# A three-stage attention and mixer kernel: decoding raw 64-bit weights in rows of 512 columns instead of 256

## Chip, cores and metric

One core of one Trainium2 chip runs the whole kernel as one program. The metric is the device time of an execution in microseconds (us). Three runs of the kernel before took 825.0, 825.81 and 827.83 us; the median is 825.81 us.

## What is computed

The reference has three stages on a tensor of 4 batches, 768 positions and 512 channels. The first is a chunked local attention (8 heads of 64 channels, 8 memory keys). The second is a gated mixture of 4 causal attention experts. The third, which the change touches, is a mixer and a two-layer network:

```python
xt = x.transpose(0, 2, 1)
h = xt @ U @ V
u = x + h.transpose(0, 2, 1)
ch = np.maximum(u @ w_ch1, 0.0) @ w_ch2       # w_ch1: 512 x 2048, w_ch2: 2048 x 512
return (u + ch).astype(np.float32)
```

`U`, `V`, `w_ch1` and `w_ch2` are 64-bit floats, which reach the chip as raw bits: two 32-bit words for each element.

## The kernel before, in words

**Numbers.** Nearly every product is made from two parts of each factor: a rounded high part (`hi`, type fp32r) and the remainder (`lo`). A product is three matmuls: lo by hi, hi by lo, hi by hi.

**Decode.** A raw weight is fetched as pairs of words (L130, or ahead of time by `fetch`, L140) and rebuilt into fp32 by `decode` (L126): one ScalarE activation scales the high word (L134), and three VectorE operations shift it (L135), put in the sign (L136) and the low bits (L137). `decode_split` (L157) then makes `hi` by a ScalarE copy (L159) and `lo` by a subtraction (L160) on VectorE, or on GpSimd for `w2`. Everything goes in pieces of 128 partitions by DC = 256 columns, two pieces to a weight row of 512.

**First layer.** Because the second attention's output projection `wo` stands in front of `w_ch1`, `fuse_w1` (L264) multiplies `woT` into `w_ch1` on the chip: for each of 4 column blocks j and each of 4 row blocks kt, two halves, each with 6 matmuls of 256 columns (L275), 192 in all. The result is split into `wp_h`, `wp_l` (L285, L286), the weights of the first layer (`product1`, L310). `load_wt` (L257) loads and splits `woT` by `split_load` (L250) in four pieces of 256.

**Second layer.** For the first FA = 4 row blocks of `w_ch2` it is a plain product: `load_w2` (L192) decodes and splits them, `gemm1` (L321) makes the relu of the first layer, and `gemm2` (L329) multiplies; sums go through `o` tiles to DRAM (`save_part`, L335). The other 12 row blocks are taken in pairs f = 4, 6, 8, 10, 12, 14, and with `wo` itself as a seventh pair (RES = 16), by a seven-product scheme for 2 by 2 blocks: `load_pair` (L198) decodes four blocks of 256 into one tile `hd`, and makes seven left factors from them (sums or differences, L216, then hi and lo, L218 and L219), `right` (L953) makes seven right factors, `multiply` (L1047) the products (L1053), and `OUTPUTS` says how they are added up.

**Stages.** Batch by batch, the two attentions run in rounds (`rnd`, L755). During the last batch's rounds (from about 310 us) the third stage begins behind them: `load_wt`, `fuse_w1` for j = 0, `load_w2`, and `early` (L343), the plain products of the first two column chunks, with pairs 4 and 6 (`fill`, L819). When attention has ended (about 422 us), the plain products of the other four chunks run, and `rest` (L935) makes the remaining weights beside them; from about 510 us to the end the seven-product scheme runs.

**Order.** The program is written in order of priority; a planner with a simulated timeline then fixes each engine's own order of instructions and each wait. An engine's queue runs in that order: a waiting instruction holds up those behind it. `issue_after` ties an instruction behind another in the plan, and `take(generator, n)` places so many steps of background work behind a round. All DMAs go through SP's queue.

**Buffers.** A tile with a tag shares that tag's `bufs` buffers and waits until one is free. Those that matter here: `d_t` (decode target, ND0 = 2 in the pool `dp0`), `d_r` (raw `woT`, 2), `raw64` (raw words), `hh` and `hl` (NHP = 4 each, used first for words fetched ahead, then for `gemm1`'s results), `w2h0` to `w2l3` (one each), `o` (2). `raw1` of kt = 0 isn't fetched ahead: it is decoded through `raw64` of `dp0`, a pool that is there from the start.

Of the kernel before, what the change touches and what calls it, by code (L numbers as in the profile page):

```python
# [23 lines left out]
DM = H * D  # L24
# [3 lines left out]
KT = DM // 128  # L28
# [32 lines left out]
ND0, NW0, ND1, NW1 = 2, 2, 6, 3  # L61
LATE = 12
NHP = 4
# [9 lines left out]
NSW = 3  # L73
# [8 lines left out]
NDE = 3  # L82
# [5 lines left out]
                ((0, 0), (0, 1), ADD), ((1, 0), (0, 0), SUB), ((0, 1), (1, 1), SUB))  # L88
# [3 lines left out]
           (((0, 0), ADD), ((1, 0), ADD)), (((0, 0), SUB), ((0, 1), ADD)), (((1, 1), ADD),), (((0, 0), ADD),))  # L92
# [5 lines left out]
def tile_chunk_attention__moe_attention__mixer(  # L98
# [22 lines left out]
    def f32(ap):  # L121
        return ap.bitcast(F32)
# [24 lines left out]
    def fetch_w1():  # L147
        for kt in range(1, KT):
            for i, hc in enumerate(halves):
                raw1[kt, i] = fetch(w1[kt, 0][:, hc], 'hh' if i else 'hl')  # L150

    def fetch_w2():
        for f in range(FA):
            for i, cs in enumerate(halves):
                raw2[f, i] = fetch(w2[f][:, cs], "hh" if i else "hl")
# [25 lines left out]
    nd, nw, nh, ns = [ND0], [NW0], [2], [NSW]  # L181
# [10 lines left out]
    def load_w2(f):  # L192
        w2h[f] = pa.tile([128, DM], F32R, name=f"w2h{f}", tag=f"w2h{f}", bufs=1)
        w2l[f] = pa.tile([128, DM], F32R, name=f"w2l{f}", tag=f"w2l{f}", bufs=1)
        for i, cs in enumerate(halves):
            decode_split(w2[f][:, cs], w2h[f][:, cs], w2l[f][:, cs], raw2.pop((f, i)), nc.gpsimd)

    def load_pair(f):  # L198
# [29 lines left out]
    def sum_tile():  # L228
        if in_b[0]:
            return dp0.tile([128, DC], F32, name="sw0", tag="w1_h", bufs=NW0)  # L230
        return dp.tile([128, DC], F32, name="sw", bufs=ns[0])

    def factor_tiles(f):

        if f < LATE:
            t = [(ea if f in EPAIRS else wp2).tile([128, 2, DC], F32R, name=f"sw{f}_{n}") for n in range(7)]
        elif f == LATE:
            t = [pa.tile([128, 2, DC], F32R, name=f"sw{f}_{n}", tag=f"w2{'hl'[n % 2]}{n // 2}", bufs=1) for n in range(7)]
        elif f == RES:
            t = [dp0.tile([128, 2, 2, DC], F32R, name=f"swr{n}", tag=f"wp_{n}0", bufs=1) for n in "hl"]  # L240
            t = [x[:, i] for x in t for i in range(2)]
            t += [ea.tile([128, 2, DC], F32R, name=f"swr{n}", tag="o", bufs=2) for n in range(2)]
            t += [pa.tile([128, 2, DC], F32R, name="swr2", tag="w2l3", bufs=1)]
        else:
            t = [pa.tile([128, 2, DC], F32R, name=f"sw{f}_{n}", tag="h" + "hl"[n % 2], bufs=NHP) for n in range(7)]
        return [(x[:, 0], x[:, 1]) for x in t]

    in_b = [False]
# [15 lines left out]
    def fuse_w1(ps, j, tag):  # L264

        acc = [ps.tile([128, 512], F32, name="w1p", **tag) for _ in range(2)]
        for kt in range(KT):
            for i, hc in enumerate(halves):
                w1_h = dp.tile([128, DC], F32R, name="w1_h", tag="w1_h", bufs=nw[0])
                w1_l = dp.tile([128, DC], F32R, name="w1_l", bufs=nw[0])  # L270
                decode_split(w1[kt, j][:, hc], w1_h, w1_l, raw1.pop((kt, i), None) if j == 0 else None)
                for pr in range(2):
                    cs = slice(pr * 128, (pr + 1) * 128)
                    for n, (w, x) in enumerate(((wt["l"], w1_h), (wt["h"], w1_l), (wt["h"], w1_h))):
                        nc.tensor.matmul(acc[pr][:, hc], w[:, kt, cs], x, start=(kt == 0 and n == 0 and i == 0),  # L275
                                         stop=(kt == KT - 1 and n == 2 and i == 1))
                if i == 0:
                    yield
            if kt < KT - 1:
                yield  # L280
# [54 lines left out]
    def save_part(po, c, m):  # L335
        o = ea.tile([128, CT], F32, name="o", tag="o", bufs=2)
# [28 lines left out]
    with ExitStack() as p1:  # L365
# [446 lines left out]
        def close_proj():  # L812
# [4 lines left out]
            nd[0], nw[0], nh[0], ns[0] = NDE, 1, NHE, NSE  # L817
# [110 lines left out]
    nd[0], nw[0], nh[0], ns[0] = ND1, NW1, 2, NSW  # L928
    with ExitStack() as p2:
# [49 lines left out]
        for c in late:  # L979
            nxt = c + 1 if c + 1 < NCH else None  # L980
            po = [ps.tile([128, CT], F32, name=f"po{m}", tag=f"po{m}", bufs=1) for m in range(KT)]
            for f in range(FA):
# [6 lines left out]
                if nxt is None and f == FS:  # L989
# [4 lines left out]
                    dp, in_b[0], nd[0], nw[0] = dp0, True, ND0, NW0  # L994
# [177 lines left out]
```

## Time and profile before

| | |
|---|---|
| median of three runs | 825.81 us |
| profiled execution, its own time | 825.71 us |
| its span, first to last instruction | 823.9 us |
| PE (TensorE matmul) busy | 795.0 us, 96% |
| DVE (VectorE) busy | 626.0 us, 76% |
| ACT (ScalarE) busy | 502.1 us, 61% |
| POOL (GpSimd) busy | 157.5 us, 19% |
| matmul line of `fuse_w1` (L275) in the chain that ended last | 2% |

The span is 1.8 us shorter than the execution's own time; that remainder lies around it. A busy share is an average over stages with different limits, so the rows below are taken stage by stage. PE's granted clock is 1.00 of full speed in every stretch used here.

### The profile page before, as it was taken

What the parts mean: (1) busy time and instruction counts of PE and PEld (TensorE: products, weight loads), DVE (VectorE), ACT (ScalarE), POOL (GpSimd) and SP (SyncE); (2) the same over time, 40 slices, a digit from 0 to 9 for tenths busy, and PEclk for the clock granted to TensorE, in tenths of its full rate; (3) what the DMA queues carried; (4) which work ended last, traced back from release to release, by engine and by line L of the source; (5) the groups of instructions that cost most, each with busy time, mean ns of one, the idle gap of its engine ahead of it and who ended that gap; (6) DMA issues with size and microseconds to landing.
All of it is one profiled execution on the core that took longest, in us unless ns stands there. A gap on an engine that the chain in (4) does not pass through costs nothing.

```text
span 823.9 us, 17920 instructions
## 1 busy us (share of the span) xinstructions
PE 795.0 (96%) x6388; PEld 717.2 (87%) x6388; DVE 626.0 (76%) x1982; ACT 502.1 (61%) x1476; POOL 157.5 (19%) x247
## 2 busy tenths in 40 slices
PE   7989999999999998899999999999999999999997
PEld 5879989989989897777878888999999999999996
DVE  4687868777677768888758699989587595784956
ACT  5787757767667745765536567665465464654652
POOL 2554434435243434441100000000000000000000
PEclk9999999999999999999999999999999999999999
DMA  9834523433233105133417544202103021030211
GB/s 287 222 117 144 169 64 96 148 104 112 64 102 104 43 2 191 47 111 115 141 36 272 179 154 158 74 1 89 41 1 128 1 78 51 1 129 1 78 52 52
DMA packets 38664, 81.53 MB, mean 99 GB/s; under 512 B 4400, under 2 KB 8496, under 8 KB 37808
## 3 DMA queue, kind: packets, MB, share of 16 engines
q1 hardware_dynamic: 38576, 80.39, 30.5%
q8 instruction: 51, 0.84, 0.4%
q14 instruction: 37, 0.30, 0.1%
HBM read 64.64 MB, written 15.73 MB: 98 GB/s over the span
## 4 chain that ended last, share of the span: by engine, by line
PE 76%; DVE 11%; DMA 5%; ACT 4%; issue 3%; POOL 1%; SPq 0%; DVEq 0%; ACTq 0%; POOLq 0%
PE acc L1053 24%; PE ph L317 15%; PE t L751 7%; PE pqk L532 6%; PE po L333 5%; PE pv L572 4%; PE s L473 4%; PE tpc L674 3%; PE sc L612 2%; PE w1p L275 2%; PE tp L501 2%; PE sc L613 2%; DMA raw<-in_w 1%; DMA k_t<-in_kw 1%; ACT ac L629 1%
## 5 line engine op out<-in xcount | busy, mean ns | idle before, releaser
L1053 PE MATMUL acc<-xhi,sw 128*128 128x256 f32 x1008 | 188.3, 282 | 0.1
L1053 PEld LDWEIGHTS acc<-xhi,sw 128*128 128x128 f32 x1008 | 159.3, 189 | 4.7 <-ACT xhi L971 0.3
L1053 PE MATMUL acc<-xlo,sw 128*128 128x256 f32 x504 | 139.0, 282 | 0.2 <-DVE xlo L972 0.2
L968 DVE TENSOR_TENSOR sx<-t 128x256 f32<-128x256 f32 x180 | 68.0, 424 | 68.2 <-ACT t L961 68.2
L961 ACT ACTIVATE t<-ph 128x512 f32<-128x512 f32 x72 | 43.1, 599 | 105.5 <-PE ph L317 105.5
L1053 PEld LDWEIGHTS acc<-xlo,sw 128*128 128x128 f32 x504 | 95.6, 190 | 2.5 <-DVE xlo L972 0.4
L654 POOL TENSOR_SCALAR ac<-ac,su,g 128x128 f32<-128x128 f32 (+5 forms) x92 | 66.9, 736 | 135.0 <-DVE su L652 50.0
L629 ACT ACTIVATE ac<-sc,nmc 128x128 f32<-128x128 f32 (+5 forms) x96 | 60.6, 635 | 43.2 <-DVE nmc L647 30.6
L971 ACT CAST xhi<-sx 128x256 fp32r<-128x256 f32 x205 | 74.7, 406 | 19.8 <-DVE sx L968 17.1
L480 ACT ACTIVATE a<-a,nm 128x96 f32<-128x96 f32 x192 | 69.9, 366 | 17.5 <-DVE nm L477 17.0
L972 DVE TENSOR_TENSOR xlo<-sx,xhi 128x256 fp32r<-128x256 f32 x205 | 77.3, 425 | 2.9 <-ACT xhi L971 2.3
L317 PE MATMUL ph<-zh,wp_l 128*128 128x512 f32 x192 | 61.2, 399 | 0.0
L317 PE MATMUL ph<-zh,wp_h 128*128 128x512 f32 x192 | 60.7, 394 | 0.0
L473 PE MATMUL s<-k_t,q_t 128*128 128x96 f32 x384 | 52.8, 275 | 6.2 <-DMA k_t<-in_kw 3.2
L473 PEld LDWEIGHTS s<-k_t,q_t 128*128 128x128 f32 x384 | 48.6, 193 | 8.8 <-DVE nm L477 4.0
L485 POOL TENSOR_TENSOR a<-a,rs 128x288 f32<-128x288 f32 x64 | 42.6, 667 | 71.7 <-DVE rs L484 34.8
L317 PE MATMUL ph<-zl,wp_h 128*128 128x512 f32 x176 | 56.1, 394 | 0.1
L674 PE MATMUL tpc<-ident_s,ac 128*128 128x128 f32 x336 | 51.7, 276 | 2.8 <-ACT ac L629 1.4
L612 PE MATMUL sc<-kl,qs 128*128 128x384 f32 (+2 forms) x144 | 48.3, 341 | 3.3 <-DVE ath L677 1.6
L477 DVE CUSTOM_DVE_ANT_0 a<-s,band_s 128x96 f32<-128x96 f32 x192 | 39.5, 251 | 14.6 <-PE s L473 14.1
L647 DVE TENSOR_REDUCE nmc<-sc 128x1 f32<-128x512 f32 (+2 forms) x48 | 39.0, 818 | 13.0 <-PE sc L616 12.5
L751 PE MATMUL t<-ath,vt 128*64 128x128 f32 x672 | 46.0, 276 | 1.9 <-DVE ath L677 1.7
(187 smaller groups left out, 1976.8 us busy)
## 6 DMA issues: line engine op xcount, KB each, us to landing
raw<-in_w SPq DMA_DIRECT2D x64, 256.0 KB, 3.5
q_t<-in_qT SPq DMA_DIRECT2D x32, 384.0 KB, 3.2
k_t<-in_kw SPq DMA_DIRECT2D x32, 288.0 KB, 3.7
v_t<-in_vw SPq DMA_DIRECT2D x32, 288.0 KB, 3.1
part<-o SPq DMA_DIRECT2D x24, 256.0 KB, 2.5
pt<-part SPq DMA_DIRECT2D x6, 1024.0 KB, 4.8
out<-pt SPq DMA_DIRECT2D x24, 256.0 KB, 2.3
zf<-zs SPq DMA_DIRECT2D x8, 512.0 KB, 4.9
```

Source lines behind the costliest of these rows:

```text
L317: nc.tensor.matmul(p, w[f // 4][:, pr, fs], z[:, pr], start=(n == 0), stop=(n == 5))
L473: last = nc.tensor.matmul(s[:, j, :], w["q"][:, qd * 3 + j], w["k"][:, qd * 3 + j], start=True, stop=True).ins
L480: nc.scalar.activation(a[:, j, :], a[:, j, :], AF.Exp, bias=nm[:, j:j + 1], scale=-1.0, accum_out=ss[:, j:j + 1])
L612: nc.tensor.matmul(s[:, o:o + w], q, kl[b, e, hf][:, :w], start=True, stop=False)
L629: nc.scalar.activation(aa[h][:, :n], src, AF.Exp, bias=nm[:, h:h + 1], scale=1.0, accum_out=su[:, h:h + 1])
L654: (nc.vector if ending[0] else nc.gpsimd).tensor_scalar(aa[h][:, :n], aa[h][:, :n], su[:, h:h + 1], gates[b, i // 3][:, i % 3, 2 * pr + h: ...
L674: hold['t', 6 * (i // 3) + 3 * pr + i % 3] = nc.tensor.transpose(tp[h][:, j * 128:(j + 1) * 128], aa[h][:, j * 128:(j + 1) * 128], ident_s ...
L751: session.append(nc.tensor.matmul(*a, **kw).ins)
L968: nc.vector.tensor_tensor(x, t[:, p[0], p[1]], t[:, q[0], q[1]], op=op)
L971: nc.scalar.copy(hi, x)
L972: nc.vector.tensor_sub(lo, x, f32(hi))
L1053: ended[0] = nc.tensor.matmul(acc[n][:, m], w[:, ms], x, start=(f == FA and u == 0 and m == 0), stop=(f == NF - 2 and u == 2 and m == 1)).ins
```

## The change

Raw rows are decoded 512 columns at a time. `fetch` takes whole rows; `raw1` now covers kt = 0 too. `d_t` of `dp0` becomes a 512 wide tile, and `split_load` uses the same two buffers for raw `woT`. `fuse_w1` makes 6 matmuls of 512 columns for each (j, kt), 96 in all; for j = 0 its `w1_h`, `w1_l` lie in the tiles that `w2h`, `w2l` take later. `gemm1` lays out its results in pairs of f, so that a pair of tiles has the size of a raw row (NHP goes from 4 to 2). For the pairs 4, 6, 8 and 10 `load_pair` decodes two rows instead of four blocks, and makes the left factors in four steps, three of them two factors wide; factor 6 changes its sign, and `OUTPUTS` takes it back. Pairs 12, 14 and 16 go as before. The `o` tiles become three.

```diff
-ND0, NW0, ND1, NW1 = 2, 2, 6, 3
+ND0, NW0, ND1, NW1, NR1, NRE = 2, 2, 3, 3, 3, 2
-NHP = 4
+NHP = 2
+NO = 3
-NSW = 3
+NSW = 2
-NDE = 3
+NDE = 2
...
     def fetch(src, tag):
-        raw = pa.tile([128, DC, 2], U32, name="raw", tag=tag, bufs=NHP)
+        raw = pa.tile([128, DM, 2], U32, name="raw", tag=tag, bufs=NHP)
...
     def fetch_w1():
-        for kt in range(1, KT):
-            for i, hc in enumerate(halves):
-                raw1[kt, i] = fetch(w1[kt, 0][:, hc], 'hh' if i else 'hl')
+        for kt in range(KT):
+            raw1[kt] = fetch(w1[kt, 0], 'hh' if kt % 2 else 'hl')
...
     def decode_split(src, hi, lo, raw=None, eng=None):
-        v = decode(dp, src, DC, raw=raw, bufs=nd[0])
+        t = dp.tile([128, DM], U32, name="d_t", bufs=nd[0])
+        v = decode(dp, src, DM, t, raw=raw, bufs=nr[0])
...
-        for i, cs in enumerate(halves):
-            decode_split(w2[f][:, cs], w2h[f][:, cs], w2l[f][:, cs], raw2.pop((f, i)), nc.gpsimd)
+        decode_split(w2[f], w2h[f], w2l[f], raw2.pop(f), nc.gpsimd)
...
+        if f < LATE:
+            for k in range(2):
+                row = hd[:, 2 * k:2 * k + 2].rearrange("p a c -> p (a c)").bitcast(U32)
+                decode(dp, w2[f + k], DM, row, bufs=nr[0])
+                yield
+            pool = ea if f in EPAIRS else wp2
+            for u, (ns_, x, y, op) in enumerate((((5, 6), hd[:, 1::2], hd[:, 0::2], SUB), ((4, 1), hd[:, 0:2], hd[:, 2:4], ADD),
+                                                 ((2, 3), hd[:, 0::3], None, None), ((0,), hd[:, 0:1], hd[:, 3:4], ADD))):
+                w = len(ns_)
+                z = pool.tile([128, 2, w, DC], F32R, name=f"sw{f}_{u}")
+                if op:
+                    v = dp.tile([128, 2, DC], F32, name="sw", bufs=ns[0])[:, :w]
+                    nc.vector.tensor_tensor(v, x, y, op=op)
+                else:
+                    v = x
+                nc.scalar.copy(z[:, 0], v)
+                nc.vector.tensor_sub(z[:, 1], v, f32(z[:, 0]))
...
     def split_load(src, hi, lo):
-        for cs in halves:
-            raw = dp.tile([128, DC], F32, name="d_r", bufs=nd[0])
-            nc.sync.dma_start(raw, src[:, cs])
-            nc.vector.tensor_copy(hi[:, cs], raw)
-            nc.gpsimd.tensor_sub(lo[:, cs], raw, f32(hi[:, cs]))
+        raw = dp.tile([128, DM], F32, name="d_r", tag="d_t", bufs=nd[0])
+        nc.sync.dma_start(raw, src)
+        nc.vector.tensor_copy(hi, raw)
+        nc.gpsimd.tensor_sub(lo, raw, f32(hi))
...
-            for i, hc in enumerate(halves):
-                w1_h = dp.tile([128, DC], F32R, name="w1_h", tag="w1_h", bufs=nw[0])
-                w1_l = dp.tile([128, DC], F32R, name="w1_l", bufs=nw[0])
-                decode_split(w1[kt, j][:, hc], w1_h, w1_l, raw1.pop((kt, i), None) if j == 0 else None)
-                for pr in range(2):
-                    cs = slice(pr * 128, (pr + 1) * 128)
-                    for n, (w, x) in enumerate(((wt["l"], w1_h), (wt["h"], w1_l), (wt["h"], w1_h))):
-                        nc.tensor.matmul(acc[pr][:, hc], w[:, kt, cs], x, start=(kt == 0 and n == 0 and i == 0),
-                                         stop=(kt == KT - 1 and n == 2 and i == 1))
-                if i == 0:
-                    yield
+            if j:
+                w1_h, w1_l = (dp.tile([128, DM], F32R, name=f"w1_{n}", bufs=NW1) for n in "hl")
+            else:
+                w1_h, w1_l = (pa.tile([128, DM], F32R, name=f"w1_{n}", tag=f"w2{n}{kt}", bufs=1) for n in "hl")
+            decode_split(w1[kt, j], w1_h, w1_l, None if j else raw1.pop(kt))
+            yield
+            for pr in range(2):
+                cs = slice(pr * 128, (pr + 1) * 128)
+                for n, (w, x) in enumerate(((wt["l"], w1_h), (wt["h"], w1_l), (wt["h"], w1_h))):
+                    nc.tensor.matmul(acc[pr], w[:, kt, cs], x, start=(kt == 0 and n == 0), stop=(kt == KT - 1 and n == 2))
...
-        hh = pa.tile([128, CT], F32R, name="hh", tag="hh", bufs=NHP)
-        hl = pa.tile([128, CT], F32R, name="hl", tag="hl", bufs=NHP)
+        if f % 2 == 0:
+            hs[c] = [pa.tile([128, 2, CT], F32R, name=n, tag=n, bufs=NHP) for n in ("hh", "hl")]
+        hh, hl = (x[:, f % 2] for x in hs[c])
```

## Rows read from the trace of the kernel before

**Rows 1.** Busy time by stretch: stretch, length, then PE, PEld, DVE, ACT, POOL busy, clock, DMA

```profile
85.00:110.00 25.00, 23.56 (x234) 21.90 (x232) 21.11 (x94) 18.52 (x68) 11.32 (x16) 1.00 0.41 129
310.00:365.00 55.00, 48.02 (x378) 41.20 (x378) 48.06 (x125) 35.51 (x103) 26.82 (x39) 1.00 0.31 101
365.00:420.00 55.00, 52.76 (x357) 42.93 (x354) 43.15 (x93) 28.78 (x67) 6.97 (x7) 1.00 0.38 123
420.00:800.00 380.00, 379.92 (x2532) 347.80 (x2531) 293.70 (x777) 215.31 (x518) 0.00 (x0) 1.00 0.24 83
```

**Rows 2.** Timeline of PE, 310 to 420 us, matmuls that waited: first, costliest, last of 17

```profile
313.20 0.33 PE L612 MATMUL sc<-kl,qs 128*128 128x128 f32 x1 [1.56 <-DVE ath L677]
...
341.35 0.30 PE L674 MATMUL tpc<-ident_s,ac 128*128 128x128 f32 x1 [1.37 <-ACT ac L629]
...
415.71 1.31 PE L751 MATMUL t<-ath,vt 128*64 128x128 f32 x20 [0.18 <-DVE ath L677]
```

**Rows 3.** Chain that ended last, in order of time: start, us, what and how many

```profile
422.70 2.78 PE ph L317 x12
...
427.84 4.11 PE po L333 x18
...
442.54 1.91 PE w1p L275 x16
...
512.88 1.40 PE ph L317 x6
```

**Rows 4.** Groups by line and shape: count, busy us, mean ns of one, idle before

```profile
L326 DVE SCALAR_TENSOR_TENSOR hl<-ph,hh 128x512 fp32r<-128x512 f32 x24 | 16.5, 691 | 6.6 <-ACT hh L325 6.4
L136 DVE SCALAR_TENSOR_TENSOR d_t<-raw,d_t 128x256 uint32<-128x256 uint32 x40 | 17.7, 452 | 0.3
L134 ACT ACTIVATE d_t<-raw 128x256 f32<-128x256 f32 x40 | 16.8, 437 | 6.9 <-DVE w_l L160 2.7 <-DVE hl L326 2.2 <-issue 0.7
L160 DVE TENSOR_TENSOR w_l<-d_t,w_h 128x256 fp32r<-128x256 f32 x32 | 13.5, 432 | 1.4 <-ACT w_h L159 1.3
L135 DVE TENSOR_SCALAR d_t<-d_t 128x256 uint32<-128x256 uint32 x40 | 13.4, 337 | 4.4 <-ACT d_t L134 4.3
L159 ACT CAST w_h<-d_t 128x256 fp32r<-128x256 f32 x32 | 12.5, 407 | 6.8 <-PE w1p L275 4.3 <-DVE d_t L137 1.5 <-DVE su L652 0.9
L134 ACT ACTIVATE hd<-raw 128x256 f32<-128x256 f32 x24 | 10.0, 433 | 10.5 <-DMA raw<-in_w 10.3
L160 POOL TENSOR_TENSOR w2l<-d_t,w2h 128x256 fp32r<-128x256 f32 x8 | 6.2, 775 | 5.2 <-ACT w2h L159 5.2
L410 POOL TENSOR_TENSOR wvg_l<-raw,wvg_h 128x520 fp32r<-128x520 f32 x2 | 2.6, 1306 | 0.0
L405 ACT CAST wqk_h<-raw 128x512 fp32r<-128x512 f32 x4 | 2.4, 610 | 2.6 <-DMA raw<-in_wqk 2.6
```

**Rows 5.** Timeline of all engines, 84 to 104 us, around the decode of kt = 0

```profile
92.48 0.43 DVE L136 SCALAR_TENSOR_TENSOR d_t<-raw,d_t 128x256 uint32<-128x256 uint32 x1
...
94.11 0.56 DVE L552 SCALAR_TENSOR_TENSOR qs<-pqk,qs 64x384 fp32r<-64x384 f32 x1
...
94.81 0.94 PE L532 MATMUL pqk<-xl,wqk_h 128*128 128x384 f32 x4 [0.67 <-DVE qs L552]
```

**Rows 6.** Timeline of all engines, 308 to 325 us: decode of kt = 1, then the split of woT

```profile
311.90 0.52 DVE L135 TENSOR_SCALAR d_t<-d_t 128x256 uint32<-128x256 uint32 x1 [0.78 <-ACT d_t L134]
...
312.34 0.81 DVE L677 COPY ath<-tpc 128x640 f32<-128x640 f32 x1
...
321.47 1.42 POOL L255 TENSOR_TENSOR wt_l<-d_r,wt_h 128x256 fp32r<-128x256 f32 x2 [3.09 <-DVE wt_h L254]
```

**Rows 7.** Timeline of all engines, 335 to 368 us: first-layer weights of j = 0

```profile
337.68 1.11 ACT L285 CAST wp_h<-w1p 128x512 fp32r<-128x512 f32 x2
...
354.15 1.27 DVE L286 TENSOR_TENSOR wp_l<-w1p,wp_h 128x512 fp32r<-128x512 f32 x2
```

More of the change, by code (lines that the diff above doesn't have):

```diff
@@ L180, in tile_chunk_attention__moe_attention__mixer @@
     dp0 = dp = pass_b.enter_context(tc.tile_pool(name="dp0", bufs=1, side="right"))
-    nd, nw, nh, ns = [ND0], [NW0], [2], [NSW]
+    nd, nr, nh, ns = [ND0], [1], [2], [NSW]
     DC = 256
@@ L194, in load_w2 @@
         w2l[f] = pa.tile([128, DM], F32R, name=f"w2l{f}", tag=f"w2l{f}", bufs=1)
-        for i, cs in enumerate(halves):
-            decode_split(w2[f][:, cs], w2h[f][:, cs], w2l[f][:, cs], raw2.pop((f, i)), nc.gpsimd)
+        decode_split(w2[f], w2h[f], w2l[f], raw2.pop(f), nc.gpsimd)
     def load_pair(f):
@@ L206, in load_pair @@
                     blk[i, k] = hd[:, 2 * k + i]
+        if f < LATE:
[15 more added lines that the diff above has]
+                nc.vector.tensor_sub(z[:, 1], v, f32(z[:, 0]))
+                for j, n in enumerate(ns_):
+                    sw[f, n] = z[:, 0, j], z[:, 1, j]
+            yield
+            return
         for k in range(2) if f != RES else ():
@@ L228, in sum_tile @@
     def sum_tile():
-        if in_b[0]:
-            return dp0.tile([128, DC], F32, name="sw0", tag="w1_h", bufs=NW0)
-        return dp.tile([128, DC], F32, name="sw", bufs=ns[0])
+        return dp0.tile([128, DC], F32, name="sw0", bufs=NW0)
     def factor_tiles(f):
-        if f < LATE:
-            t = [(ea if f in EPAIRS else wp2).tile([128, 2, DC], F32R, name=f"sw{f}_{n}") for n in range(7)]
-        elif f == LATE:
+        if f == LATE:
             t = [pa.tile([128, 2, DC], F32R, name=f"sw{f}_{n}", tag=f"w2{'hl'[n % 2]}{n // 2}", bufs=1) for n in range(7)]
@@ L241, in factor_tiles @@
             t = [x[:, i] for x in t for i in range(2)]
-            t += [ea.tile([128, 2, DC], F32R, name=f"swr{n}", tag="o", bufs=2) for n in range(2)]
+            t += [ea.tile([128, 2, DC], F32R, name=f"swr{n}", tag="o", bufs=NO) for n in range(2)]
             t += [pa.tile([128, 2, DC], F32R, name="swr2", tag="w2l3", bufs=1)]
         else:
-            t = [pa.tile([128, 2, DC], F32R, name=f"sw{f}_{n}", tag="h" + "hl"[n % 2], bufs=NHP) for n in range(7)]
+            t = [pa.tile([128, 2, 2, DC], F32R, name=f"sw{f}_{n}", tag="h" + "hl"[n % 2], bufs=NHP) for n in range(4)]
+            t = [x[:, i] for x in t for i in range(2)][:7]
         return [(x[:, 0], x[:, 1]) for x in t]
-    in_b = [False]
     def split_load(src, hi, lo):
-        for cs in halves:
-            raw = dp.tile([128, DC], F32, name="d_r", bufs=nd[0])
-            nc.sync.dma_start(raw, src[:, cs])
-            nc.vector.tensor_copy(hi[:, cs], raw)
-            nc.gpsimd.tensor_sub(lo[:, cs], raw, f32(hi[:, cs]))
+        raw = dp.tile([128, DM], F32, name="d_r", tag="d_t", bufs=nd[0])
+        nc.sync.dma_start(raw, src)
+        nc.vector.tensor_copy(hi, raw)
+        nc.gpsimd.tensor_sub(lo, raw, f32(hi))
     def load_wt():
@@ L335, in save_part @@
     def save_part(po, c, m):
-        o = ea.tile([128, CT], F32, name="o", tag="o", bufs=2)
+        o = ea.tile([128, CT], F32, name="o", tag="o", bufs=NO)
         if m % 2 or wp2 is not None:
@@ L816, in close_proj @@
             dp = dpe.enter_context(tc.tile_pool(name="dpe", bufs=1, side="right"))
-            nd[0], nw[0], nh[0], ns[0] = NDE, 1, NHE, NSE
+            nd[0], nr[0], nh[0], ns[0] = NDE, NRE, NHE, NSE
         def fill():
```

11 lines of the change are left out of this document (6 added, 5 removed).

## The prediction

> **What bounds the kernel now.** I read busy time by stretch first [rows 1]. From 420 to 800 us PE is busy 379.92 of 380 us: nothing that DVE, ACT or the DMAs save there can show, and only fewer or shorter matmuls shorten it. In the last batch's attention PE is idle 6.98 us of 55 (310 to 365) and 2.24 us of 55 (365 to 420), with DVE busy 48.06 and 43.15 us. From 85 to 110 us, where the decode of kt = 0 lies, it is idle 1.44 us of 25. The change touches no other stretch, so what it can give beside PE's own work is at most 1.44 + 6.98 + 2.24 = 10.7 us. Second, PE's waits in the timeline [rows 2]: 17 between 310 and 420 us, nearly all on DVE or ACT work of the attention, the longest 1.56 and 1.37 us. Third, the chain of waits in order of time [rows 3], for the pace of matmuls without gaps. Fourth, the groups by shape [rows 4], for the price of each operation at 256 and 512 columns.
>
> **The sum, part by part.** It is made against the profiled execution's own 825.71 us (span 823.9 and 1.8 around it), 0.1 below the median of 825.81.
>
> **Matmuls of fuse_w1.** Removed are 192 of 256 columns at 1.91 / 16 = 119.4 ns, 22.9 us; added are 96 of 512. Their pace is that of the nearest rows: 4.11 / 18 = 228, 2.78 / 12 = 232, 1.40 / 6 = 233 ns [rows 3]. I take 230, so 22.1 us: 0.8 us less; ends 0.5 and 1.0. It shows whole, since PE is the bound where j = 1 to 3 run, and j = 0 lies in PE's queue too. 96 weight loads go as well; they run beside matmuls.
>
> The Trainium skill (TensorE: Matmul & The Clock Gate, Back-to-back issue gap) gives the isolated gap as columns over 2.4 plus 2.5 ns. By that the term would be 96 x 2.5 ns = 0.24 us, an estimate from that page. The rows' 119.4 and 230 ns give more, and decide.
>
> **Prices of the wide decode.** A piece of 256 costs DVE 337 + 452 and about 452 again, 1.24 us, and 432 ns for `lo` [rows 4]. At 512 an operation with two inputs takes 691 ns. The shift has no row at 512: it lies between its own 337 and 691; I take 337 plus half the 259 ns by which the others grow, 0.47, because at 256 it is already 100 ns cheaper than they are. So a wide row costs 0.47 + 2 x 0.69 = 1.85 us against 2.48, and with `lo` 2.54 against 3.35. ACT: 2 x (437 + 407) = 1.69 us becomes about 1.25, from the 610 ns cast of 512 and the 30 ns by which the activation on raw words is dearer. POOL's subtraction goes from 2 x 775 to 1306 ns.
>
> **kt = 0 moves.** Before, its two halves were decoded at 91 to 98 us through a pool that is there from the start: 3.35 us of DVE, 1.7 of ACT. Now its words go into tiles that exist only after the local attention, so its DMA joins SP's queue at 308 us. At 94.11 to 94.81 PE waits 0.67 us for an attention operation that stood behind several decode operations [rows 5]; without them it goes, and some of the other 0.77 us of idle time with it. I take 1.0 us; ends 0 and 1.44.
>
> **A new wait: decode behind the split of woT.** Raw `woT` and decode now share two buffers. `woT` arrives early and holds both until POOL has subtracted. The split before ran from 321.47 [rows 6]; one wide subtraction of 1.31 us frees the first buffer at about 322.8. So kt = 0 and kt = 1, of which kt = 1 was decoded from 311 us on, begin at 322.8. Behind ACT's and DVE's waits stand attention operations, unless the planner puts them in front, as its simulated time allows. What goes: at 311.90 a decode shift kept DVE until `ath` began at 312.34, and PE waited 1.56 us for that [rows 2, 6]. I take 0.6 us off (0.44 plus part of ACT's similar turn); ends 0 and 1.56. What comes: 2.5 us of decode move behind 322.8 and 3.35 us of kt = 0 are new in the stretch. Against 6 pieces of w1 before (10.0 us) stand 4 wide rows (10.2); for w2 four rows (7.4) against eight pieces (9.9). DVE's load from 321 to 365 us is then about what it was (10.2 + 7.4 after; 20 less 2.5 before), so I put no change on the 5.4 us that PE is idle there (6.98 less 1.56); ends 2.0 less, and 4.4 more (second rival).
>
> What waits for w1: `wp_h` is written from 337.68, `wp_l` only from 354.15 [rows 7]. The first layer could not begin before, so j = 0 has some 15 us to spare; later w1 matmuls cost nothing while that lasts. SP's queue: words of w2 wait for the decoded rows of w1 and hold up stores of z and loads for the first chunks behind them; those z stores have no reader until later, and w2 has the same 15 us. `w2h` tiles wait for w1's matmuls of the same kt, which lie ahead anyway.
>
> **Pairs 4 and 6 (365 to 420 us).** Each pair saves DVE 2 x 0.63 for the rows, 5 x 432 against 2 x 691 + 432 for the sums (0.35) and 7 x 432 against 3 x 691 + 432 for `lo` (0.52): 2.1 us, 4.2 for both, a tenth of DVE's 43.15 us; ACT saves about 2.2 us in all. ACT also stood 10.3 us, over all pairs, behind raw words not yet landed [rows 4]; two whole-row buffers hold a pair. PE's idle 2.24 us should shrink by some 0.9; ends 0 and 2.24.
>
> **The rest.** For j = 1 to 3 and pairs 8 and 10 DVE saves 12 x 0.81 + 2 x 2.1 = 14 us, ACT some 7, all under PE's full queue [rows 1]: nothing. `gemm1`'s tiles in pairs free a buffer up to one f later; PE has other products in between: nothing, and some 0.7 us (three matmuls of 230 ns) for each early f if not. The third `o` tile, the sign of factor 6 and other pool sizes: nothing, hidden by the same matmuls.
>
> Sum: 0.8 + 1.0 + 0.6 + 0.9 = 3.3 us less, 825.7 - 3.3 = 822.4 us.
>
> **Rivals.** *Only PE's term shows.* PE's order is fixed by the plan, and a gap closed in front of one matmul opens at the next, since attention is a chain from score to maximum to exponential to transpose. For it: DVE is busy at 87% from 310 to 365 us and PE's 17 waits are mostly short. Against it: two of the waits named have a decode operation directly in front. Time: 825.7 - 0.8, with some reshuffling 824.9.
>
> *Wide operations stand in front of attention (slower).* From 321 to 420 us DVE's queue takes a decode operation whenever attention has nothing ready; an attention operation that comes then waits up to 691 instead of 432 ns. If each of the 17 waits of PE grows by that 0.26 us, 4.4 us are added: 825.7 + 4.4 - 0.8 - 1.0 = 828.3. It decides if wide operations stand directly in front of most of PE's waits; if in front of half, it cancels the other gains. For it: 312.34 shows just that form [rows 6]. Against it: there are half as many of them.
>
> The Trainium skill (SBUF — State Buffer, Who interferes with whom) says that a DVE operation with two SBUF inputs and a GpSimd operation reading SBUF shut each other out for the whole instruction. By that, POOL's six wide subtractions would lengthen a wait by up to 1306 - 775 = 531 ns each, 3.2 us in all, on the same side; no row here separates it.
>
> *Most of the gaps close.* If DVE's relief also takes half of the 5.4 us at 321 to 365, all of 365 to 420 and all of 85 to 110: 825.7 - 0.8 - 1.4 - 0.6 - 2.7 - 2.2 = 818.0. For it: a list of waits on one busy engine can shorten together. Against it: DVE's load at 321 to 365 is not smaller.
>
> **How the numbers follow.** Forecast 0.45, only PE's term 0.30, slower 0.15, most gaps close 0.10. A measurement of this kernel can tell about 0.3%, 2.5 us, from no change. The forecast's own bounds (821 to 824.5) cross that line at 823.3: of its 0.45 about 0.35 lie below, and 0.10 above. Faster: 0.35 + 0.10 and a little of the second case, 0.47; slower: most of the third, 0.13; same: 0.40. The range reaches from 819.0, near the fourth case, to 827.0, half way to the slower one; outside lie about half of the fourth and most of the third case. The sum is for the profiled execution; the median stands 0.1 above it, so 822.4 serves for both.
>
> **What would show it.** Right: 96 matmuls on `w1p` at about 230 ns; no decode near 90 us, and PE's wait at 94.8 gone; first `d_t` activation of j = 0 after 322 us; the idle time of PE at 310 to 420 us below 8.5; DVE busy about 24 us less (16 x 0.81 + 4 x 0.63 + 4 x 2.1); 420 to 800 still full. Wrong: PE idle at 310 to 420 us above 9.2, with waits whose DVE or POOL operation stood behind a 512 wide one; `wp_l` or the first layer later than 356 us; or PE no longer full after 420.

## The result, and the profile after

The changed kernel takes 832.23 us (median of 8 runs, 829.98 to 837.15), the kernel before beside it 827.14: ratio 1.0065, interval 1.0042 to 1.0088. It is slower, and above the range of the prediction (819.0 to 827.0). Its profiled execution took 831.31 us (span 829.4), 5.6 more than the one the sum was made against. DVE's busy time fell by 10.2 us (626.0 to 615.8), ACT's by 5.7.

The same stretches as in [rows 1], of the kernel after, with two more (columns as there; the eighth is the granted clock):

```profile
0.00:30.00 30.00, 24.50 (x184) 19.29 (x186) 15.85 (x95) 17.74 (x72) 6.34 (x14) 0.89 0.99 290
85.00:110.00 25.00, 24.52 (x236) 22.93 (x233) 19.29 (x88) 18.42 (x64) 11.65 (x17) 1.00 0.41 128
310.00:365.00 55.00, 47.02 (x335) 39.02 (x334) 45.37 (x102) 34.09 (x89) 26.75 (x30) 0.97 0.29 101
365.00:420.00 55.00, 53.97 (x369) 44.45 (x368) 40.39 (x70) 29.49 (x61) 9.09 (x10) 1.00 0.37 130
460.00:512.00 52.00, 48.99 (x208) 37.96 (x207) 43.30 (x84) 28.71 (x56) 0.00 (x0) 1.00 0.54 172
420.00:800.00 380.00, 376.99 (x2433) 340.14 (x2432) 289.73 (x706) 209.69 (x482) 0.00 (x0) 1.00 0.24 82
```

The fifth of them in the kernel before:

```profile
460.00:512.00 52.00, 51.92 (x281) 44.58 (x280) 46.12 (x130) 34.82 (x87) 0.00 (x0) 1.00 0.48 163
```

Three things stand out. PE's idle time at 85 to 110 us is nearly gone, as forecast. (From 310 to 420 us it is 9.0 us, between the prediction's two signs, below 8.5 and above 9.2.) The stretch that was full has lost 3 us, all of it between 460 and 512 us. And the clock was at its half level (1.2 GHz) in 0.22 of the first 30 us and in 0.06 of 310 to 365 us.

Because those half-clock times move everything behind them, I compare lengths between the starts of the same events of PE's and ACT's work, not times of day: A from the sixth copy of `vt` on ACT to the 21st, B on to the first `po` matmul, C to the 97th (the first of chunk 2), D to the first `acc` matmul, E to the last.

| us | start to A | A | B | C | D | E |
|---|---|---|---|---|---|---|
| before | 86.4 | 214.9 | 66.0 | 60.4 | 82.4 | 303.0 |
| after | 88.9 | 213.6 | 66.7 | 60.3 | 86.1 | 303.0 |

The gain is in A (1.3 us); the loss is 2.6 us ahead of A, 0.7 in B and 3.7 in D.

Where D's time went, in the chain of waits of the kernel after, 425 to 520 us in order of time (start, us, what): its pieces that are transfers.

```profile
434.78 1.90 DMA zs<-z
438.95 6.57 DMA raw<-in_w
...
452.88 4.77 DMA raw<-in_w
...
466.19 4.38 DMA raw<-in_w
...
474.14 4.23 DMA raw<-in_w
...
493.64 5.32 DMA part<-o
```

The four `raw` pieces are 20.0 us of the chain; before, the same stretch of the chain was PE's matmuls, but for 5.8 us from 498.6 us on (a transfer of `wo` and DVE's work behind it), and no transfer of raw words stood in it. A transfer in the chain is not a loss by its length, since PE works on beside it: PE's waits there are 2.9 us in all. How a raw word reaches PE is seen in the timeline of the kernel after:

```profile
470.59 0.66 ACT L135 ACTIVATE hd<-raw 128x512 f32<-128x512 f32 x1 [1.60 <-DMA raw<-in_w]
471.15 0.58 ACT L339 ACTIVATE hh<-ph 128x512 fp32r<-128x512 f32 x1
...
471.78 1.47 PE L347 MATMUL po<-hh,w2l 128*128 128x512 f32 x3 [0.74 <-ACT hh L339]
...
498.32 0.43 ACT L135 ACTIVATE hd<-raw 128x256 f32<-128x256 f32 x1 [3.21 <-DMA raw<-in_w]
...
499.04 0.59 ACT L352 COPY o<-po 128x512 f32<-128x512 f32 x1 [0.28 <-DMA part<-o]
...
499.68 0.50 PE L347 MATMUL po<-hh,w2l 128*128 128x512 f32 x1 [0.94 <-ACT o L352]
```

ACT takes its work in order. `hh`, which PE waits for, stands behind a decode step whose raw words have not landed; so does the copy `o`, which frees PE's accumulator. That `o` then waits 0.28 us more, for the store of an earlier `o` (`part`), the last piece of the chain above, which SP issued just behind a fetch of raw words. In 425 to 520 us ACT waits for raw words this long in all (engine, line, waited for: us, times, longest):

```profile
ACT d_t L135 <- DMA raw<-in_w: 7.5, 5, 2.9
...
ACT hd L135 <- DMA raw<-in_w: 7.4, 3, 3.2
```

In B the longest wait of PE has grown from 1.56 us [rows 2] to 2.74. Its timeline, DVE, POOL and PE of the kernel after:

```profile
342.78 1.28 POOL L160 TENSOR_TENSOR w2l<-d_t,w2h 128x512 fp32r<-128x512 f32 x1 [0.41 <-ACT w2h L159]
...
343.14 1.47 DVE L138 SCALAR_TENSOR_TENSOR d_t<-raw,d_t 128x512 uint32<-128x512 uint32 x1
...
344.64 0.96 DVE L652 TENSOR_REDUCE nmc<-sc 128x2 f32<-128x768 f32 x1
...
345.34 1.27 POOL L160 TENSOR_TENSOR w2l<-d_t,w2h 128x512 fp32r<-128x512 f32 x1 [1.28 <-ACT w2h L159]
...
345.63 1.06 DVE L735 CAST qm<-qf 32x128 fp32r<-32x128 f32 x1
...
347.04 0.16 DVE L589 COPY lg<-pv 128x4 f32<-128x4 f32 x1
...
347.25 0.39 PE L586 MATMUL pv<-wvg_h,xl 128*128 128x260 f32 x1 [2.74 <-DVE lg L589]
```

`d_t` takes 1.47 us beside POOL's subtraction where it takes 0.69 alone, and the small `qm` 1.06; the clock falls to half at 356.2 us, 9 us after the wait. That the wait brings this isn't shown: in early_only, an experiment below, the clock falls at 330.9 us and the same wait ends only at 348.4.

**Time against the clock.** Each run lists its mean granted clock. Over the 136 runs of the kernel before that stand beside the experiments (median 828.7 us, mean clock 0.9942), time falls on a line: 825.8 us at clock 1.0 and 0.52 ± 0.05 us more for each 0.001 less, with a scatter of 1.1 us. The 155 runs of the kernels whose early half is wide have the same slope, 0.52, each taken about its own kernel's mean. "At full clock" below is a kernel's mean time taken to 1.0 at that slope, with its 95% half width, in which the slope's own uncertainty is left out. The kernel after stands at 827.2 ± 0.5 (20 runs, mean clock 0.9909). The mean of these runs lies 3.2 us above the mean of before: 1.5 are there at full clock, and 1.7 (0.0033 of clock) are half clock.

### The profile page after: what moved, and what is told of

Same layout as the page of the kernel before. It is cut to its first block, busy times and chain, and to the rows that moved or that the text cites. A ratio compares the mean times of both kernels' runs of the same rounds, so it can differ in the third digit from the quotient of the medians.

```text
span 829.4 us, 17451 instructions
## 1 busy us (share of the span) xinstructions
PE 798.0 (96%) x6292; PEld 714.8 (86%) x6292; DVE 615.8 (74%) x1860; ACT 496.4 (60%) x1416; POOL 159.8 (19%) x241
## 4 chain that ended last, share of the span: by engine, by line
PE 78%; DVE 8%; DMA 5%; ACT 3%; issue 3%; POOL 1%; SPq 0%; DVEq 0%; ACTq 0%; POOLq 0%
PE acc L1067 24%; PE ph L330 14%; PE t L765 8%; PE pqk L546 7%; PE s L487 4%; PE po L347 4%; PE pv L586 4%; PE tpc L688 3%; PE sc L626 3%; DMA raw<-in_w 2%; PE tp L515 2%; PE sc L627 2%; DMA k_t<-in_kw 1%; DVE d_t L138 1%; ACT ac L643 1%
## 5 line engine op out<-in xcount | busy, mean ns | idle before, releaser
L668 POOL TENSOR_SCALAR ac<-ac,su,g 128x128 f32<-128x128 f32 (+5 forms) x92 | 70.1, 771 | 130.5 <-DVE su L666 43.2
```

The source lines that it names most:

```text
L668: (nc.vector if ending[0] else nc.gpsimd).tensor_scalar(aa[h][:, :n], aa[h][:, :n], su[:, h:h + 1], gates[b, i // 3][:, i % 3, 2 * pr + h: ...
```

## The experiments

**after_again**: the changed kernel itself.

> The changed kernel once more, as a control beside the three others. If the half clock that its trace shows from 14.9 to 21.7 us (worth 2.6 us by the shift of the first projections) is chance, this trace has none there and a time of about 829.5; if it belongs to the program, it is there again at the same place and the time is again about 832. In either case the stage from 435 to 553 us costs about 3.7 us more than before, and the biggest wait of PE between 310 and 365 us is above 2 us at the vt product.

Measured: 831.38 us, 1.0044 (1.0026 to 1.0063) of before. D is 86.3 us long, PE's wait at `pv` again 2.72. Half clock stands at 11.2 us for 6.8 and at 345.7 and 355.9 for 3.4 each.

**early_only** and **late_only** cut the change in two at 420 us; the `o` tiles stay two in both.

```
early_only, against the kernel after:
-ND0, NW0, ND1, NW1, NR1, NRE = 2, 2, 3, 3, 3, 2
+ND0, NW0, ND1, NW1, NRE = 2, 2, 6, 3, 2
...
-        if f < LATE:
+        if f in EPAIRS:
...
+                for i, hc in enumerate(halves):
...
+                    decode_half(w1[kt, j][:, hc], w1_h, w1_l)
late_only, against the kernel before:
-ND0, NW0, ND1, NW1 = 2, 2, 6, 3
+ND0, NW0, ND1, NW1, NR1 = 2, 2, 3, 3, 3
...
+                decode_row(w1[kt, j], w1_h, w1_l)
...
+        if f in (8, 10):
...
+                decode(dp, w2[f + k], DM, row, bufs=NR1)
```

> The changed kernel with the late stage as before: the first layer's blocks 1 to 3 and pairs 8 and 10 decoded in 256 columns with six buffers of raw words; what stays wide is the w2 tiles, block 0, the raw output weights and pairs 4 and 6. Theory 1 (the cost lies in the late stage, where three raw buffers of 512 KB make ACT wait in order): 3 to 4 us less than the changed kernel, so 826 to 829, PE's busy time from 420 to 512 us back to 91.9, and raw words that end less than 1 us of ACT's idle there at d_t. Theory 2 (the cost lies at 310 to 360 us, where block 0 is decoded in one run): no more than 1 us less than the changed kernel, so 830 to 832, the 2.7 us wait of PE at 347 us still there. Theory 3 (the cost is the clock's dip at the start): the same as the changed kernel where that dip is there, and 829.5 where it is not.

> The kernel before with the late stage alone made wide: blocks 1 to 3 of the first layer and pairs 8 and 10 in rows of 512 columns, three raw buffers, left factors two at a time; everything up to 420 us as before. Theory 1: 3 to 4 us above the kernel before, so 829 to 832, with ACT waiting 10 us or more on raw words from 425 to 555 us and PE idle more than 2 us between 460 and 500. Theory 2: within 1 us of the kernel before, 826 to 828, and PE as full there as before. Theory 3: as the kernel before, unless its trace shows the dip at the start.

Measured: early_only 828.07, ratio 1.0023 (0.9998 to 1.0049), at full clock 824.2 ± 0.9; D 82.1 us, and PE had no wait from 425 to 520 us. late_only 833.64, ratio 1.0068 (1.0034 to 1.0102), at full clock 829.8 ± 0.8; D 87.9, in which late_only also ran at half clock for 3.4 us from 502.2 us on. PE from 460 to 512 us, early_only, then late_only:

```profile
460.00:512.00 52.00, 52.00 (x278) 44.56 (x277) 47.49 (x132) 34.75 (x86) 0.00 (x0) 1.00 0.50 165
460.00:512.00 52.00, 47.89 (x199) 37.97 (x199) 42.53 (x83) 28.34 (x55) 0.00 (x0) 0.97 0.59 182
```

The loss lies in the late half: the early half alone is 1.6 us faster than before at full clock (824.2 against 825.8), and the late half costs 3.0 on top of it (827.2 against 824.2), and 4.0 on the kernel before (829.8). early_only's median does not show it, because its runs had the lowest clock so far (mean 0.9894).

**late_fine, pairs_narrow, w1_narrow**: which piece of the late half?

```
late_fine, against the kernel after:
-        v = decode(dp, src, DM, t, raw=raw, bufs=nr[0])
...
+            for cs in halves:
+                decode(dp, src[:, cs], DC, t[:, cs], bufs=2 * nr[0])
pairs_narrow, against the kernel after:
-        if f < LATE:
+        if f in EPAIRS:
w1_narrow, against the kernel after:
-            decode_split(w1[kt, j], w1_h, w1_l, None if j else raw1.pop(kt))
...
+                for i, hc in enumerate(halves):
...
+                    v = decode(dp, None, DC, t[:, hc], raw=piece)
+                    nc.scalar.copy(w1_h[:, hc], v)
```

> The changed kernel, in which the late stage takes its raw words and decodes them in halves of 256 columns (six buffers of 256 KB in place of three of 512 KB, the same memory); the casts, the subtractions, the first layer's matmuls and the left factors of pairs 8 and 10 stay 512 wide. If the late stage's loss is the grain of the raw words (ACT stands in order behind a 512 KB transfer), it is gone: PE busy 51 us or more from 460 to 512 us (changed kernel 49.0 and 48.6, early_only 52.0), ACT's waits for raw words in 425 to 520 us down from 14.9 to 8 us or less, time 2 to 4 us below the changed kernel of the same clock. If it is the 512-wide operations of DVE and ACT that stand in front of hh and hl, PE stays below 50 us there and the time is within 1 us of the changed kernel's.

> The changed kernel with pairs 8 and 10 alone as before: raw rows decoded in halves (two transfers into the same 512-wide buffers), left factors one at a time; blocks 1 to 3 stay wide. If the loss of 3 to 4 us comes from the pairs (the three longest waits of ACT for raw words, 1.6, 2.6 and 3.2 us, are the pairs'), PE is busy 51 us or more from 460 to 512 us and the time falls by 2 to 4 us; if it comes from the blocks of the first layer, PE stays at about 49 us there and the time within 1 us; if from both, about 50.5 us and half of it.

> The changed kernel with blocks 1 to 3 of the first layer alone in halves again (two transfers into the same buffers, operations and matmuls of 256 columns); pairs 8 and 10 stay wide. The counterpart of pairs_narrow: whatever of the loss in 460 to 512 us that kernel does not give back is given back here (PE 51 us or more and 2 to 4 us less if the blocks are the cause, 49 us and within 1 us if the pairs are); against that, 72 matmul pairs of 119 ns in place of one of 230 ns cost 0.6 us of PE.

Measured: 831.95, 834.37, 833.85 us; at full clock 827.0 ± 0.5, 828.3 ± 1.2, 828.4 ± 0.7. D is 85.7, 88.3 (with 3.4 us of half clock from 478.7 us on), 88.0 and PE's busy time in 460 to 512 us 48.33, 47.57, 47.18. All three expectations of a cure failed: neither the grain of the raw words, nor the pairs, nor the blocks alone is the cause. In pairs_narrow PE's longest wait is 2.45 us from 474.5 on, among the blocks; in w1_narrow 4.5 us are lost at 491 to 501, among the pairs. What they share with the kernel after is a ring only three rows deep (in late_fine the raw words of three rows, in six halves). By its expectation late_fine pointed at the 512-wide operations in front of `hh` and `hl`; the next two runs keep these.

**ring_raw5, ring_both**: the depth of the rings.

```
-ND0, NW0, ND1, NW1, NR1, NRE = 2, 2, 3, 3, 3, 2
ring_raw5:
+ND0, NW0, ND1, NW1, NR1, NRE = 2, 2, 3, 3, 5, 2
ring_both:
+ND0, NW0, ND1, NW1, NR1, NRE = 2, 2, 5, 3, 4, 2
```

> The changed kernel with five buffers of 512 KB for raw words in the late stage in place of three; nothing else. late_fine, pairs_narrow and w1_narrow each gave back none of the late loss, early_only all of it; what the three share with the changed kernel is a ring of rows only three deep (raw words or decoded words) in front of in-order queues. If the depth of the raw ring is the cause (SP's raw fetches wait 18.0 us for DVE's last read, and the stores behind them), PE is busy 51 us or more from 460 to 512 us, against 49.0 and 48.6, and the time is 2 to 4 us less at the same clock. If the depth of the decoded ring or the width of the operations is the cause, PE stays at 48 to 49.5 us and the time within 1 us.

> The changed kernel with five buffers for decoded rows and four for raw rows in the late stage in place of three and three. If either ring's depth is the cause, PE is busy 51 us or more from 460 to 512 us; with ring_raw5 unchanged that puts it on the decoded ring (ACT waits 3.7 us for w_l's read of the slot). If both kernels stay at 49 us, no ring is the cause, and what is left is the order in which the 512-wide work stands in front of hh and hl on ACT and DVE.

PE from 460 to 512 us in ring_raw5:

```profile
460.00:512.00 52.00, 51.50 (x227) 42.18 (x226) 43.41 (x85) 30.36 (x58) 0.00 (x0) 1.00 0.45 152
```

and ACT's waits for raw words there, 425 to 520 us:

```profile
ACT hd L135 <- DMA raw<-in_w: 3.3, 3, 2.1
```

3.3 us in place of 14.9, and the chain's raw pieces are down from four to one of 4.62 us. D is 81.6 us, less than the 82.4 before, and 82.9 in ring_both. In ring_both ACT still waits 10.3 us for raw words, and PE only 1.3 us: what counts is what stands behind such a wait, not the sum. At full clock ring_raw5 stands at 823.1 ± 0.8 and ring_both at 824.2 ± 0.9, 4.1 and 3.0 below the kernel after. The medians (829.41 and 829.79, ratios 1.0020 and 1.0008, both with 1 inside the interval) hide it: ring_raw5's profile had half clock at 15.1, 346.2 and 359.9 us, 20.4 us in all. The late loss hangs on the depth of the raw ring: two more whole rows cure it, with all widths and other pool sizes as they were. With the depth the planned order of PE and SP in the late stage changes too; no run tells the two apart.

**early_w2l_dve, early_w2l_half**: POOL beside DVE in B.

```
early_w2l_dve, against early_only:
-        decode_split(w2[f], w2h[f], w2l[f], raw2.pop(f), nc.gpsimd)
+        decode_split(w2[f], w2h[f], w2l[f], raw2.pop(f))
early_w2l_half, against early_only:
-        (eng or nc.vector).tensor_sub(lo, v, f32(hi))
+        for cs in halves if eng else (slice(0, DM),):
+            (eng or nc.vector).tensor_sub(lo[:, cs], v[:, cs], f32(hi)[:, cs])
```

> early_only with the four 512-wide low parts of w2 subtracted on DVE in place of POOL. In all six traces with block 0 wide, PE waits 1.4 to 2.7 us for pv's lg near 345 us and the clock falls to half for 3.4 us or more at 331 to 360 us; in the three with block 0 narrow, neither. There DVE's operations stretch beside POOL's 1.28 us subtraction (d_t 1.47 for 0.69 us, qm 1.06 for 0.28). If that contention is the cause, the wait falls below 1 us, no half clock is left from 320 to 365 us, and the time is 1 to 2.5 us below early_only's at the same clock at the start. If DVE's load is the cause, 2.8 us more of it make the wait 2 us or longer and the dip stays.

> early_only with each of POOL's four 512-wide subtractions for w2's low part in two halves of 256 columns, still on POOL. If one long hold of POOL is what lengthens DVE's operation in front of lg, the wait near 345 us falls below 1 us and the half clock from 320 to 365 us is gone; if the total of both counts and not its length, the wait stays at 1.4 us or more, with the dip.

The same operations in early_w2l_dve, where POOL no longer subtracts:

```profile
341.19 0.67 DVE L138 SCALAR_TENSOR_TENSOR d_t<-raw,d_t 128x512 uint32<-128x512 uint32 x1
...
342.88 0.22 DVE L758 CAST qm<-qf 32x128 fp32r<-32x128 f32 x1
...
344.17 0.69 DVE L160 TENSOR_TENSOR w2l<-d_t,w2h 128x512 fp32r<-128x512 f32 x1
344.77 0.15 DVE L612 COPY lg<-pv 128x4 f32<-128x4 f32 x1
...
344.98 0.39 PE L609 MATMUL pv<-wvg_h,xl 128*128 128x260 f32 x1 [1.21 <-DVE lg L612]
```

0.67 for 1.47 us and 0.22 for 1.06: the contention is shown. But PE's wait is 1.21 us, not below 1, since `lg` now stands behind the subtraction on DVE itself. Its median is 827.31 (0.9982, 0.9958 to 1.0006). early_w2l_half kept a wait of 2.06 us and half clock at 349.6, so halves do not help: median 828.49 (0.9999). At full clock the two stand at 823.4 ± 0.6 and 824.1 ± 0.8, no measurable step from early_only.

**before_again, before_third**: the kernel before, one profile each.

> The kernel before, once more with a profile. Its runs lie between 825.6 and 831.9 us with granted clocks from 1.0 to 0.989. If the half clock in the first 30 us that all four other kernels show is chance, it can show here as well (on the record of the runs, about one time in two), between 10 and 25 us, and then the shift of the projections after it is half its length; if it belongs to the new code alone, there is none.

> The kernel before, a third profile. If the half clock between 320 and 365 us belongs to block 0 in wide rows, there is none here, as in the two profiles before and in late_only; if it comes by chance to either, this may show one.

830.0 and 826.82 us. The first has half clock at 11.2 us for 13.7, the second at 13.4 for 3.4; neither has any from 320 to 365 us. Both lost it at the start, so that half clock at the start is no property of the change, and the profile that the sum was made against, with none ahead of its last 2 us (PE has no work left there), was one of the quickest of this kernel: clock 0.999 where the runs' mean is 0.994.

**ring_w2l_dve, ring_w2_narrow**: both remedies, then the half clock of B.

```
ring_w2l_dve, against ring_raw5:
-        decode_split(w2[f], w2h[f], w2l[f], raw2.pop(f), nc.gpsimd)
+        decode_split(w2[f], w2h[f], w2l[f], raw2.pop(f))
ring_w2_narrow, against ring_raw5:
-        decode_split(w2[f], w2h[f], w2l[f], raw2.pop(f), nc.gpsimd)
...
+        for cs in halves:
...
+            nc.gpsimd.tensor_sub(w2l[f][:, cs], v, f32(w2h[f][:, cs]))
```

> The changed kernel with both causes mended: five raw buffers in the late stage (ring_raw5) and the low parts of w2 subtracted on DVE (early_w2l_dve). ring_raw5 stands at 822.7 us on the line of its runs against the clock where the kernel before stands at 825.6, but loses it to half clock at 346 to 360 us; early_w2l_dve's trace had none there. If the two add, the median is 825 to 827, 2 to 4 us below the kernel before, PE is above 51 us in 460 to 512 us and no half clock stands from 320 to 365 us. If the half clock comes with any block 0 in wide rows, it is there again, and the median is within 1.5 us of the kernel before.

> ring_raw5 with the four w2 tiles decoded and split in halves of 256 columns (each fetched in one transfer of 512 KB as in the changed kernel), POOL subtracting as before; block 0 stays wide. If the wide w2 rows, on DVE and POOL, are what holds pv's lg back, PE's wait near 345 us falls from 2.7 to about 1.4 us or less, as at the same place before; if it is the bunching of block 0, it stays above 2 us with the half clock behind it. Time between 825 and 829 by the clock.

825.48 us, ratio 0.9960 (0.9940 to 0.9979), and 825.66, ratio 0.9965 (0.9943 to 0.9988): both beat the kernel before, by 0.4%; at full clock 820.7 ± 0.4 and 820.8 ± 0.5. ring_w2l_dve is 2.4 below ring_raw5, where the same edit took 0.8 off early_only, within its noise; why it gives more here isn't shown. In ring_w2_narrow the wait at `pv` is gone (the longest left near there is 0.55 us until 352 us). Yet both have half clock in B, at 323.2 and 347.1, and at 331.5 and 355.4. In ring_w2l_dve PE's waits over 0.25 us from 310 to 366 us are 4.8 us, less than the 6.2 before:

```profile
310.00:365.00 55.00, 49.49 (x340) 40.94 (x339) 45.93 (x105) 34.55 (x91) 21.09 (x26) 0.94 0.29 101
```

**kt0_early, kt0_second, block0_narrow**: the first row of block 0, or its width? All three start from ring_w2l_dve.

```
kt0_early, against ring_w2l_dve:
-        for kt in range(KT):
+        for kt in range(1, KT):
...
+                for hc in halves:
+                    decode(dp, w1[kt, j][:, hc], DC, t[:, hc], bufs=nd[0])
block0_narrow, against ring_w2l_dve:
+            if j == 0:
...
+                for i, hc in enumerate(halves):
+                    v = decode(dp, None, DC, t[:, hc], raw=raw[:, hc])
+                    nc.scalar.copy(w1_h[:, hc], v)
```

> ring_w2l_dve with the first row of block 0 taken out of the joint fetch again: its raw words come by two transfers of 256 columns into the buffers of the small ring, as in the kernel before, so that it can be decoded long before 320 us and its 512-wide matmuls can start as soon as the split weights are there (before: 12 matmuls from 322.4 us on; ring_w2l_dve: the first at 329.6 us, and 17 PE instructions from 320 to 325 us against 33 to 48 in the kernels without half clock). If the missing early matmuls are what lets the clock fall, the first block-0 matmul starts before 325 us, and no half clock stands from 320 to 365 us, and the time is 1.5 to 3 us below ring_w2l_dve at the same clock at the start; the gap that its decode made at 94 us (0.67 to 1.15 us) may come back. If the bunched decode of the other three rows is the cause, the half clock is there again near 345 us and the time within 1 us of ring_w2l_dve's 825.5.

> kt0_early once more with a profile, a second look at whether the half clock between 320 and 365 us is gone there: its first profile had none although its first block-0 matmul came only at 327.9 us, 1.7 us earlier than in ring_w2l_dve. If that was chance, as it can have been in early_w2l_dve, one stands here.

> ring_w2l_dve with block 0 alone decoded, split and multiplied in halves of 256 columns again (its four rows still fetched in 512 KB transfers, decoded from 321 us on). If it is the 512-wide operations of block 0 that bring the half clock between 320 and 365 us, there is none here, the runs' mean clock rises from 0.992 to about 0.995 (the kernel before's) and the time stays at 824 to 826 us in spite of 24 matmul pairs of 119 ns for one of 230 (0.2 us). If it is that row 0 of block 0 is decoded at 321 us and no longer at 91, whatever its width, the half clock is there again and the mean clock stays at 0.992 or below.

kt0_early: 824.32 us, ratio 0.9956 (0.9934 to 0.9977), the best median; 822.1 ± 0.9 at full clock, mean clock 0.9945. B in its profile:

```profile
310.00:365.00 55.00, 48.05 (x347) 39.46 (x346) 46.78 (x109) 35.06 (x93) 22.59 (x28) 1.00 0.26 91
```

No half clock there, and none in kt0_second (823.27 us). But row 0 was decoded at 321 us all the same, and the first `w1p` matmul came at 327.9 us: the condition I had set (before 325) was not met. block0_narrow: 828.07, ratio 0.9983 (0.9961 to 1.0005), mean clock 0.9924, half clock at 342.6 us and a wait of 2.99: the width of block 0 is not what brings it. PE's waits from 310 to 366 us are 9.1 us here, and at full clock it stands at 824.4 ± 0.6, 3.7 above ring_w2l_dve. Over all traces, 12 of 13 with row 0 in the joint fetch show half clock in B, and none of 6 without (three of before, late_only, two of kt0_early). Why the place of that fetch should do it stays open: PE's total idle time there does not separate them. A pair of buffers for the raw output weights alone, so that row 0 could start before POOL's split (own_dr), has no time: one pool wants 6 KB of each partition, and 5.97 are left.

## Why the prediction was wrong

Its sum, term by term:

- **Matmuls of fuse_w1** (0.8 less): right, a little small. After 420 us two `w1p` matmuls of 512 start 227 ns apart, two of 256 before 120: 96 x 13 = 1.2 us. Where the ring is deep enough it shows: D is 81.6 and 81.5 us in ring_raw5 and ring_w2l_dve against 82.3 to 82.4 in the three profiles before.
- **Prices of the wide decode** (DVE busy about 24 us less): wrong, two to three times too large. DVE's busy time fell by 10.2 us. The prediction set the length of one operation at 512 columns against two lengths at 256, but operations in a row overlap at their ends. Two low parts of `w_ch1` in a row, before and after:

```profile
470.61 0.76 DVE L160 TENSOR_TENSOR w_l<-d_t,w_h 128x256 fp32r<-128x256 f32 x2
466.03 1.29 DVE L160 TENSOR_TENSOR w_l<-d_t,w_h 128x512 fp32r<-128x512 f32 x2
```

One alone lasts 0.42 and 0.68 us, so that they start some 0.34 and 0.60 us apart, and a wide one in place of two frees some 0.07 us of DVE, not the 0.17 to 0.21 that were priced. By the median start-to-start times (335 and 602 ns, the shift 202 and 336) the whole saving is about 8 us, an estimate, and that of pairs 4 and 6 is 1.5 us in place of 4.2.

- **kt = 0 moves** (1.0 less): right. A is 214.9, 215.4 and 215.8 us in the three profiles before and 213.5 or 213.6 in all with the early half wide. The wait at 94.81 [rows 5] (0.67, 1.16 and 1.62 us in the three) is gone, and PE's idle time at 85 to 110 us is 0.48.
- **The decode behind the split of woT** (0.6 less, 321 to 365 no change): the wait was right; the price of the stretch is open. Decode's first shift is at 323.67 us in the kernel after, behind POOL's split, as worked out; the wait of 1.56 at 313.20 [rows 2] shrank to 0.29. B is 66.0 us before, 64.2 to 64.5 in the three profiles of the wide kernels without half clock there, and 65.3 to 70.4 with it; 66.7 in the kernel after. All three without it have the low part of w2 on DVE, so no profile shows what B takes at full clock in the kernel after. The forecast had no term for the clock, and all of [rows 1] read 1.00.
- **Pairs 4 and 6** (0.9 less): the idle time shrank, 2.24 to 1.03 us in 365 to 420, but the first two chunks came no sooner: C is 60.4, 59.7 and 60.3 us before and 59.8 to 60.4 in the profiles with the early half wide. The time went to other work of PE's, which moved here from B: C has 414 matmuls for 398, B 432 for 472 (24 of these 40 are gone because block 0 of `fuse_w1` has 24 of 512 for 48 of 256). So B and C are better read together: 125.7 to 126.5 us in the three profiles before, 127.0 in the kernel after, and 124.5 to 124.8 in the three without half clock.
- **The rest** (nothing): this step failed, at "other pool sizes: nothing, hidden by the same matmuls". From PE busy 379.92 of 380 us [rows 1] I concluded that nothing there can show. That a full queue hides a saving does not mean that it hides a loss. Three whole rows in place of six halves are the same bytes, and I priced them so; but with whole rows three deep, ACT waited 14.9 us for raw words (7.5 and 7.4) and PE 2.9 us for ACT and DVE. D grew by 3.7 us, 3.0 at full clock by the halves of the change. At 512 columns only the depth gave it back.

Added up for the two profiles: start 2.6, A -1.3, B 0.7, C -0.1, D 3.7, together the 5.6 us between them. Of the 8.9 us between the forecast and the kernel after's profile, 2.6 are the start, where it ran at half clock for 6.8 us (two of the three profiles before have half clock there too), and 3.7 are D; the rest, 2.6, is B with its half clock, the missing term of C, and the 0.6 that D should have gained, less 0.3 that A gave beyond its term.

The rivals: the slower one named wide operations in front of attention from 321 to 420 us. Its mechanism was there (the 2.74 us wait), but in one place and not in seventeen, and B's waits in sum are 7.7 us against 6.2: 1.5 of the 4.4 it was priced at. The Trainium skill (SBUF — State Buffer, Who interferes with whom) was drawn on there for POOL and DVE shutting each other out; the traces agree for `d_t`, which ends 0.55 us after POOL's operation, and the cast `qm`, which has one input, was stretched as well, 1.06 against 0.22 us. That the loss would sit after 420 us, in a ring, no rival said; only the last sentence ("or PE no longer full after 420") did.

With the raw ring at five the change stands at 823.1 ± 0.8 us at full clock, 2.7 below the kernel before where 3.3 were forecast, and with w2's low part on DVE as well at 820.7. So at full clock most of the reckoned gain is there once the ring is five deep, and the three buffers, and then the clock, took it away. That the sum comes so near is in part luck: DVE's prices were two to three times too large, A gave more than its term, and C nothing.

## What to carry to other kernels

When transfers and operations are made twice as wide in the same memory, the ring is half as deep: count for how many of the new, wider operations it holds words (for these, three rows fetched as six halves were no better, and five rows were enough), and price what stands behind the one that is late in an in-order engine, even where the matmul engine is full. Price operations in a row by their start-to-start times, not by their lengths. A stretch with no idle time is a place where savings are hidden, not where losses are. And before a sum is made against one profile, look at where its granted clock stands among the runs.

## What the runs showed that was not expected

- The clock explains most of the spread between runs of one program: 0.52 us for 0.001 of mean clock over 136 runs, 823.66 to 834.08 us, with 1.1 us of scatter left.
- Half clock comes in the first 30 us in 16 of 19 profiles, from 3.4 to 13.7 us, in the kernel before as in the others. Between 8 and 17 us PE waits once or twice, 1 to 3 us at a time, for the transfers of the first scores' inputs; it did so too, 2.07 us, in the profile of before that kept full clock.
- In B half clock came in profiles with 4.8 us of waits and stayed away in others with 6.1 to 6.7. What triggers it is not settled.
- Rows of 256 columns do not need the deeper ring and rows of 512 do, at equal bytes (early_only, six halves: no wait of PE; after, three rows: 2.9 us); raw words in six halves for 512-wide work (late_fine) did not help either.
